# Convolution leaving two neighbouring rows in a partition, a second stage on 64-row halves and seven weight buffers in a spectral-mix kernel

## The chip, the cores and the metric

The kernel runs on one core of a Trainium2 chip. The metric is the device time of one execution in microseconds (us). Before the change the median of three runs is 230.59 us. The engines are named as in the profile: PE is the matrix engine's matmuls, PEld its weight loads (they can overlap PE), DVE the vector engine, ACT the scalar engine, POOL the general-purpose engine, which here mostly issues loads, and SP the engine that issues the stores. Every matmul result lands in PSUM, which this kernel holds as four tiles Z[0] to Z[3] of two banks each.

## The reference

Inputs: x of shape (8, 3264, 192) in float32 (B batches, S rows, D columns), weight (8, 7), and, called moe_ below, w_r and w_i (64, 192, 192) and w_ch (192, 192). In short:

```python
w = softmax(weight, axis=-1)                       # 8 heads, 7 taps
u0 = causal 7-tap convolution of x along S         # 24 columns of D per head
X = rfft(u0, axis=1)                               # along S
Y[:, :64] = complex product of X[:, :64] with w_r + i w_i, a 192x192 matrix per mode
y = irfft(Y, n=S, axis=1)
u = u0 + y
out = u + maximum(u @ w_ch, 0)                     # float32
```

Only the first 64 modes are used, so both transforms are matmuls with small cosine and sine tables. The kernel works in bf16 with float32 accumulation.

## The kernel before, in words

**Layout.** The order of instructions on each engine is the order in which the program writes them (manual_schedule); what waits for what follows from tiles that are written and read. A sequence of 3264 rows is cut into NF = 25 tiles of 128 rows and a half tile of 64; batches go in NQ = 4 pairs q, i being the batch in the pair. xall (L58) holds x, and later the convolved u0, as [128 rows, slot, i, 192].

**Stage 1: load, convolution, forward transform (L115 to L289).** load_unit (L115) loads the row tiles of a unit from x with POOL's queue, casting to bf16, with one DMA per batch of the pair (L121). The work is cut into 24 units (L47 to L49), six for each pair, of 2, 4 or 5 row tiles. The set-up builds the taps by a softmax, seven masks (L147), and a banded matrix `band` of 128 x 256 per head: L168 writes each tap into a packed form under a mask, L174 and L176 copy that to the band. The cosine and sine tables `ftab` follow: products L151, reduction L153, L158, L177 and L178 on DVE, then Sin, Abs and Sin on ACT (L180 to L182). conv_half (L219) convolves a unit for four heads: four matmuls with the main band (L228) and four with the band's spill into the next tile (L234), each with 128 output rows and n x 2 x 24 moving columns (192 for four tiles, 240 for five); L237 does the half tile. ACT (L242) or DVE (L244) copies the bank pair back into xall. conv_half uses Z[0] and Z[1], one each. dft_unit (L246) accumulates the forward transform of a unit in Z[2], one matmul of 384 columns per tile (L250; L254 for the half tile), one unit behind the convolution; when a pair is done, xtrans (L259) turns the result with twelve matmuls that use the two column halves of the array, L264 on columns 0 to 63 and L266 on 64 to 127 (`tile_position`), and DVE copies it to mixa (L271) for the mixing.

**Stage 2: mixing per mode and transposes (L292 to L390, L499 to L516).** The weights w_r and w_i come in NG = 16 groups of four modes; load_w (L294) loads one group with two DMAs on POOL's queue (L297) into one of five buffers. mix (L361) does the twelve small matmuls of a group (L366) and then issues the load of the group that takes the same buffer, g + 5. mix_copy (L371) and mix_trans (L374) bring the result to `yet`. Between the mixes stand the transposes which the last stage needs, in 49 jobs: g_bank (L318, transposes of the tables L321), cm_bank (L324, columns 0 to 127 of u0, L329, with L334 for the half tile) and ct_bank (L336, columns 128 to 191 of two batches stacked, L340, with L347 for the half tile). A job fills one bank of Z[0] or Z[1] with up to eight transposes, and one copy of 128 x 1024 takes it out: `copy` (L306) gives every third to ACT (L309), the others to DVE (L311). next_bank (L313) goes around the four banks of those two tiles. `some(4)` and `some(3)` (L508, L514) put seven jobs after each two mixes. The first matmuls of the output's first two items are put between and after the last mixes.

**Stage 3: output (L392 to L539).** An item is a duo: two row tiles of a pair of batches, one in each bank of a Z tile. z_pieces (L392) lists the matmuls of a tile: "c" is u0 @ w_ch (with `cm` and wm over 64 of the 128 columns at a time, and `ct` with wt2 for the last 64 columns), "g" is the inverse transform's contribution to u @ w_ch, with `zw`'s first half, "y" the inverse transform itself with its second half. `both` (L418) issues the pieces of the two tiles in turn on two row halves of the array, rows 0 to 63 and 64 to 127, the matmul being L436: 12 of 192 moving columns and 8 of 384 per item. When the halves swap banks, a nop (L424) waits for the last matmuls before. relu (L458, ACT) makes maximum(u @ w_ch, 0) in PSUM between the "g" and the "y" pieces, finish (L461) adds u0 (DVE, L478) into an output buffer in `arena` and stores it with two DMAs on SP, one per batch (L486) or per tile (L491). Of the seven output buffers each holds one item. zw_pair (L441) makes `zw` for one pair of batches from `yet`: four matmuls and two scaled copies (DVE L450, ACT L452). Two zw_pairs stand ahead of the loop, and two inside it after items 13 and 26 (L538). One item in the 51 takes the four half tiles together ("h").

Of the kernel before, what the change touches and what calls it, by code (L numbers as in the profile page):

```python
# [9 lines left out]
ALU = mybir.AluOpType  # L10
# [9 lines left out]
def kernel(  # L20
# [21 lines left out]
    TAIL = D - P  # L42
# [4 lines left out]
    UNITS0 = ((0, 2), (2, 4), (6, 5), (11, 5), (16, 5), (21, 5))  # L47
    UNITS = ((0, 5), (5, 5), (10, 4), (14, 4), (18, 4), (22, 4))
    units = [(q, t0, n) for q in range(NQ) for t0, n in (UNITS if q else UNITS0)]  # L49

# [6 lines left out]

    xall = sb("xall", [NSLOT, 2, D], BF16)  # L58
    cm = sb("cm", [NQ, 2 * NF + 1, P], BF16)
    ct = sb("ct", [NQ, NT, P], BF16)  # L60
    ftab = sb("ftab", [NT + 1, 2 * MODES], BF16)
    yet = sb("yet", [2, B, 2 * MODES], BF16)
    mixa = sb("mixa", [3 * (MODES + 1) * 2 * B], BF16)
    xt = mixa[:, :].rearrange("p (j m k) -> p j m k", j=3, m=MODES + 1)
    zw = mixa[:, 0:2 * B * D].rearrange("p (t b d) -> p t b d", t=2, b=B)
    band = sb("band", [H, 2 * P], BF16)
    wm = sb("wm", [2 * D], BF16)
    w1 = sb("w1", [2 * D], BF16)
    wt2 = sb("wt2", [D], BF16)
    ident = sb("ident", [P], BF16)  # L70
    perm = sb("perm", [P], BF16)
    ascale = sb("ascale", [1], F32)
    halfpi = sb("halfpi", [1], F32)
    xs = [sb(f"xs{i}", [2, D], BF16) for i in range(2)]
    ymix = [sb(f"ymix{i}", [2, D], BF16) for i in range(2)]
    NW = 5
    WGB = 4 * 3 * D
    arena = sb("arena", [NW * WGB], BF16)
    wts = [arena[:, WGB * i:WGB * (i + 1)].rearrange("p (m j e) -> p m j e", m=4, j=3) for i in range(NW)]
    NO = 7  # L80
    OB = 2 * 2 * 2 * D
    outs = [arena[:, OB * i:OB * (i + 1)].bitcast(F32).rearrange("p (k d) -> p k d", k=2) for i in range(NO)]
# [8 lines left out]
    NTM = NT + 1  # L91
    kprod = temp(NTM * MODES, F32)
    turns = temp(NTM * MODES, F32)
# [8 lines left out]
    cidx = temp(PW, F32)  # L102
    masks = temp(KK * PW, U16)
    sidx = temp(NTM, F32)
# [7 lines left out]
    def slot(q, t):  # L112
        return NT * q + t

    def load_unit(q, t0, n):  # L115
        nf = min(n, NF - t0)
        s0 = slot(q, t0) + 1
        for i in range(2):
            off = ((2 * q + i) * S + P * t0) * D
            src = bass.AP(tensor=x.tensor, offset=x.offset + off, ap=[[D, P], [P * D, nf], [1, D]])  # L120
            nc.gpsimd.dma_start(out=xall[:, s0:s0 + nf, i, :], in_=src)  # L121
# [5 lines left out]
    load_unit(*units[0])  # L127
    nc.gpsimd.iota(sidx[:, 0:NT], pattern=[[P, NT]], base=0, channel_multiplier=1,
                   allow_small_or_imprecise_dtypes=True)
    nc.gpsimd.iota(sidx[:, NT:NTM], pattern=[[1, 1]], base=P * NF - HALF, channel_multiplier=1,  # L130
                   allow_small_or_imprecise_dtypes=True)
    nc.gpsimd.iota(midx, pattern=[[1, MODES]], base=0, channel_multiplier=0,
                   allow_small_or_imprecise_dtypes=True)
    for g in range(4):
        nc.gpsimd.iota(cidx[32 * g:32 * g + 32, :], pattern=[[1, PW]], base=0, channel_multiplier=-1,
                       allow_small_or_imprecise_dtypes=True)
    load_unit(*units[1])
    hs = [xall[HALF:P, NT:NSLOT:NT, 0, :], xall[0:HALF, NT:NSLOT:NT, 1, :]]
    nc.vector.memset(halfpi[:], math.pi / 2)
    nc.vector.memset(ascale[:], 2.0 / S)  # L140
    nc.vector.memset(ascale[0:1, :], 1.0 / S)
    nc.vector.memset(ascale[64:65, :], 1.0 / S)
    for a in hs:
        nc.vector.memset(a, 0.0)
    nc.vector.memset(band[:], 0.0)
    for k in range(KK):
        nc.vector.tensor_scalar(out=masks[:, PW * k:PW * (k + 1)], in0=cidx,  # L147
                                scalar1=float(KK - 1 - k), scalar2=None, op0=ALU.is_equal)
    kp3 = kprod.rearrange("p (t m) -> p t m", t=NTM)
    tu3 = turns.rearrange("p (t m) -> p t m", t=NTM)  # L150
    nc.vector.tensor_tensor(out=kp3, in0=sidx.unsqueeze(2).to_broadcast([P, NTM, MODES]),  # L151
                            in1=midx.unsqueeze(1).to_broadcast([P, NTM, MODES]), op=ALU.mult)
    nc.vector.tensor_scalar(out=turns, in0=kprod, scalar1=1.0 / S, scalar2=MAGIC, op0=ALU.mult, op1=ALU.add)  # L153
# [4 lines left out]
    nc.vector.tensor_scalar(out=turns, in0=turns, scalar1=-MAGIC, scalar2=float(S), op0=ALU.add, op1=ALU.mult)  # L158
# [7 lines left out]
    nc.vector.memset(packed, 0.0)  # L166
    for k in range(KK):
        nc.vector.copy_predicated(out=pk3,  # L168
                                  mask=masks[:, PW * k:PW * (k + 1)].unsqueeze(1).to_broadcast([P, H, PW]),
                                  data=ta3[:, :, k:k + 1].to_broadcast([P, H, PW]))  # L170
# [6 lines left out]
    nc.vector.tensor_tensor(out=kprod, in0=kprod, in1=turns, op=ALU.subtract)  # L177
    nc.vector.tensor_scalar(out=kprod, in0=kprod, scalar1=-float(S) / 2, scalar2=float(S) / 2,  # L178
# [6 lines left out]
    for q, t0, n in units[2:5]:  # L185
        load_unit(q, t0, n)
# [12 lines left out]
    for q, t0, n in units[5:9]:  # L199
        load_unit(q, t0, n)  # L200
# [10 lines left out]
    for q, t0, n in units[9:]:  # L211
        load_unit(q, t0, n)
# [86 lines left out]

    for g in range(NW):  # L300
        load_w(g)
# [268 lines left out]
```

## Time and profile before

| what | value |
|---|---|
| runs | 231.66, 230.59, 227.48 us; median 230.59 |
| the profiled execution: span from its first to its last instruction | 230.0 us |
| mean granted PE clock | 0.916 |
| busy: PE, PEld | 167.9 us (73%), 125.9 us (55%) |
| busy: DVE, ACT, POOL | 131.1 us (57%), 96.5 us (42%), 67.5 us (29%) |
| moved | 40.03 MB, mean 174 GB/s |
| convolution L228, L234: matmuls, busy | 192 and 192, 26.4 and 26.1 us |
| forward transform L250 | 100, 20.6 us |
| output matmuls L436 | 1048 in three groups, 112.0 us |
| output add L478 on DVE | 50, mean 958 ns |
| relu L459 on ACT | 51, mean 795 ns |
| store on SP | 102, 192.0 KB each, 3.1 us from issue to landing |

The profile is one execution. Its slices cut the span into 40 equal parts of 5.75 us; a digit is the busy share of an engine in tenths (9 means 90% or more), PEclk the clock that PE was granted in tenths of full speed, DMA the mean busy share of the 16 DMA engines, GB/s what they moved. A row of the timeline gives the start of a run of equal instructions in us, the busy time, the engine, the line, the operation, output <- inputs with their shape and type, how many instructions there were (x32), and in square brackets the idle time ahead with what ended it. A row of the chain of waits gives the start, the time that the chain spent there, the engine, tile and line, and how many instructions. The chain goes back from the last instruction to whatever released it each time. Matmuls are pipelined, so the sum of their durations counts overlap; in the text their price is taken from start to start.

### The profile page before, as it was taken

The numbers are of one execution on the slowest core, as the hardware profiler recorded it, in microseconds if no ns is written. First come the engines' busy times: TensorE is split into PE (matmuls) and PEld (weight loads), VectorE is DVE, ScalarE is ACT, GpSimd is POOL, SyncE is SP. The second block draws the span as 40 slices with busy tenths as digits, with TensorE's granted clock in tenths as the row PEclk, the third lists the DMA queues.
The fourth block names the chain that finished last, engine by engine and source line by source line (L and its number), as shares of the span: only waits on it lengthen the run. The fifth ranks groups of instructions, "written<-read, shape, count | busy, mean of one in ns | idle before, by whom it ended". The sixth has DMA issues, their size and how long they took to land.

```text
span 230.0 us, 5494 instructions
## 1 busy us (share of the span) xinstructions
PE 167.9 (73%) x2303; PEld 125.9 (55%) x2303; DVE 131.1 (57%) x177; ACT 96.5 (42%) x123; POOL 67.5 (29%) x115
## 2 busy tenths in 40 slices
PE   0010999899799836665866666869989997999960
PEld 0010888688687715654755565426646655666730
DVE  6991254845758463345344452335776776877690
ACT  2039334424343310423443244236655665666540
POOL 7999996775730004044034200000000000000000
PEclk9999999999999995589589769599999999999996
DMA  3999999999999004879998860004799997799997
GB/s 43 157 184 188 190 190 191 189 192 189 173 197 206 10 0 64 144 105 153 157 136 133 146 104 0 3 0 126 246 313 286 303 308 236 240 315 310 309 276 250
DMA packets 63912, 40.03 MB, mean 174 GB/s; under 512 B 29584, under 2 KB 63888, under 8 KB 63888
## 3 DMA queue, kind: packets, MB, share of 16 engines
q0 software_dynamic: 36000, 19.59, 63.6%
q1 hardware_dynamic: 27888, 20.09, 28.3%
q8 instruction: 18, 0.29, 0.5%
q14 instruction: 6, 0.05, 0.1%
HBM read 39.20 MB, written 20.05 MB: 258 GB/s over the span
## 4 chain that ended last, share of the span: by engine, by line
PE 53%; POOL 14%; DVE 12%; DMA 10%; ACT 5%; issue 4%; DVEq 0%; POOLq 0%; ACTq 0%
PE z L436 28%; POOL xall L121 11%; DMA xall<-in_x_dram 10%; PE z L329 7%; PE z L340 4%; DVE cm L311 3%; PE z L366 3%; PE z L228 2%; DVE mixa L271 2%; PE z L234 2%; PE z L250 2%; DVE xall L244 2%; PE z L321 1%; ACT cm L309 1%; DVE ct L311 1%
## 5 line engine op out<-in xcount | busy, mean ns | idle before, releaser
L478 DVE TENSOR_TENSOR arena<-z,xall 128x768 f32<-128x768 f32 x50 | 47.8, 958 | 18.2 <-ACT z L459 10.6
L436 PE MATMUL z<-mixa,ftab 64*128 64x384 bf16 (+1 forms) x432 | 51.1, 317 | 1.7 <-ACT z L459 0.8
L459 ACT ACTIVATE z<-z 128x768 f32<-128x768 f32 x51 | 40.5, 795 | 24.5 <-PE z L436 24.5
L228 PE MATMUL z<-xall,band 128*128 128x192 bf16 (+2 forms) x192 | 26.4, 263 | 25.5 <-ACT band L174 15.1
L244 DVE CAST xall<-z 128x768 bf16<-128x768 f32 (+2 forms) x24 | 25.1, 1047 | 29.6 <-PE z L234 18.7
L121 POOL DMA_DIRECT2D xall<-in_x_dram x48 | 39.5, 840 | 6.6 <-DMA xall<-in_x_dram 5.0
L436 PE MATMUL z<-wm,cm 64*128 64x192 bf16 x408 | 34.9, 250 | 3.1 <-ACT mixa L452 2.7
L242 ACT CAST xall<-z 128x768 bf16<-128x768 f32 (+2 forms) x24 | 20.4, 851 | 34.7 <-PE z L234 24.8
L228 PEld LDWEIGHTS <-band 128*128 128x128 bf16 x192 | 17.9, 102 | 29.1 <-ACT band L174 15.1
L436 PEld LDWEIGHTS <-cm 64*128 64x128 bf16 x408 | 15.9, 95 | 24.5 <-PE z L436 14.6
L329 PE MATMUL z<-ident,xall 128*128 128x128 bf16 x208 | 19.3, 257 | 10.6 <-DVE cm L311 5.8
L297 POOL DMA_DIRECT2D arena<-in_moe_w_r_dram x16 | 10.1, 629 | 54.8 <-PE z L366 53.5
L234 PE MATMUL z<-xall,band 128*128 128x192 bf16 (+2 forms) x192 | 26.1, 257 | 0.0
L436 PE MATMUL z<-wt,ct 64*128 64x192 bf16 x208 | 26.0, 247 | 0.0
L329 PEld LDWEIGHTS <-xall 128*128 128x128 bf16 x208 | 16.4, 117 | 13.3 <-issue 12.0
L436 PEld LDWEIGHTS <-ftab 64*128 64x128 bf16 x432 | 19.7, 94 | 3.9 <-issue 2.2
L311 DVE COPY cm<-z 128x1024 bf16<-128x1024 bf16 (+1 forms) x19 | 11.7, 627 | 17.5 <-PE z L329 17.3
L250 PE MATMUL z<-xall,ftab 128*128 128x384 bf16 x100 | 20.6, 330 | 0.4 <-DVE xall L244 0.4
L234 PEld LDWEIGHTS <-band 128*128 128x128 bf16 x192 | 18.2, 102 | 0.6
L271 DVE CAST mixa<-z 128x384 bf16<-128x384 f32 x8 | 13.6, 1877 | 2.1 <-PE z L266 2.1
L340 PE MATMUL z<-ident,xall 128*64 128x128 bf16 x208 | 9.6, 245 | 6.8 <-DVE cm L334 2.9
L309 ACT COPY cm<-z 128x1024 bf16<-128x1024 bf16 (+1 forms) x9 | 9.1, 1006 | 12.7 <-PE z L329 12.7
(89 smaller groups left out, 160.8 us busy)
## 6 DMA issues: line engine op xcount, KB each, us to landing
out_dram<-arena SPq DMA_DIRECT2D x102, 192.0 KB, 3.1
arena<-in_moe_w_r_dram POOLq DMA_DIRECT2D x16, 288.0 KB, 6.0
arena<-in_moe_w_i_dram POOLq DMA_DIRECT2D x16, 288.0 KB, 6.8
xall<-in_x_dram POOLq DMA_DIRECT2D x18, 240.0 KB, 6.8
xall<-in_x_dram POOLq DMA_DIRECT2D x22, 192.0 KB, 8.4
xall<-in_x_dram POOLq DMA_DIRECT2D x6, 144.0 KB, 7.5
xall<-in_x_dram POOLq DMA_DIRECT2D x4, 96.0 KB, 4.1
wm<-in_moe_w_ch_dram POOLq DMA_DIRECT2D x1, 48.0 KB, 6.8
```

The costliest lines, as they stand in the source:

```text
L121: nc.gpsimd.dma_start(out=xall[:, s0:s0 + nf, i, :], in_=src)
L228: nc.tensor.matmul(o, band[:, h, 0:P], xall[:, s0 + 1:s0 + 1 + n, :, dsl], start=(j % 2 == 0), stop=False, skip_group_check=True)
L234: nc.tensor.matmul(o[:, k0:n, :, :], band[:, h, P:2 * P], xall[:, s0 + k0:s0 + n, :, dsl], start=False, stop=not last, skip_group_check=True)
L242: nc.scalar.copy(out=dst, in_=srcv)
L244: nc.vector.tensor_copy(out=dst, in_=srcv)
L250: nc.tensor.matmul(xp, ftab[:, t, :], xall[:, slot(q, t), :, :], start=(t == 0), stop=False, skip_group_check=True)
L311: nc.vector.tensor_copy(out=out, in_=in_)
L329: nc.tensor.transpose(tp[:, P * k:P * k + P], xall[:, slot(q, t), i, 0:P], ident[:])
L340: nc.tensor.transpose(tp[64 * i:64 * i + 64, P * k:P * k + P], xall[:, slot(q, t0 + k), i, P:D], ident[:], tile_position=(0, 64 * i))
L436: mm = nc.tensor.matmul(zt[:, bank, cols], l, r, start=(begin and k == 0), stop=(end and k == len(lst) - 1), skip_group_check=True)
L459: nc.scalar.activation(out=zt[:, :, 0:2 * D], in_=zt[:, :, 0:2 * D], func=ACT.Relu)
L478: nc.vector.tensor_tensor(out=o[:, :, :], in0=zt[:, :, 0:2 * D], in1=xall[:, s[0]:s[1] + 1:s[1] - s[0], :, :].rearrange("p k i d -> p k (i ...
```

## The change

The layout of rows changes for the whole kernel. The convolution writes row 2p + j of a group of 256 rows into partition p, slot j, so a partition holds two neighbouring rows, and the pair of rows of one batch is 1536 contiguous bytes of the output.

- Set-up: one mask in place of seven; the band is made of 32-column writes; the memset of `packed` comes ahead; the table has 26 groups instead of 27; its steps become the functions table_a to table_d, table_sin and table_cos. They are issued between the copies of the first convolution rounds. Sine and cosine are two ACT instructions each.
- Stage 1: 12 units, each of 4 or 5 groups of 256 rows, loaded by fewer and larger DMAs. conv_round does two heads at a time, four rounds per unit, with 16 matmuls of 64 output columns each, whose stationary operand is the band at stride 2, and which go to the two column halves of the array in turn. Z[0], Z[1] and Z[2] take the rounds in turn, and the copies alternate between ACT and DVE. The forward transform uses Z[3] and runs up to three units behind at the start. xtrans's two copies to mixa are in a contiguous order, one on DVE and one on ACT.
- Stage 2: the three columns 3p + j of a row are turned at a time, so that 384 columns of two batches fill three transposes of 128 x 128: ct_job, 40 jobs, and g2_job for the tables, 7 jobs, 47 in all. cm, cm_bank and ct_bank go. The stationary operand of ct_job has stride 3. Two of every five copies go to ACT. Weights have seven buffers, of which four lie in the part of `ct` that the last pair's jobs fill; wslot lists the buffer of each group, and a load is issued after the mix that used its buffer last. Two jobs, xtrans and two more jobs stand ahead of the first mix. zw is made in two halves of 32 modes each, zw_low for all four pairs after mix 9, the other half after mix 15. Mixes 14 and 15 are copied and turned singly, with the first matmuls of items 0 and 1 between.
- Stage 3: 52 items, an item being a group of 256 rows of both batches. z_c and z_y issue its 28 matmuls, all of 192 moving columns, in turn on the two row halves; each row half keeps to its own bank, and the nop goes. finish adds and stores with one DMA of 384 KB; there are six output buffers. zw_pair and the half-tile item go: the last item of each pair has 96 partitions (PT) instead of 128.

```diff
-    UNITS0 = ((0, 2), (2, 4), (6, 5), (11, 5), (16, 5), (21, 5))
-    UNITS = ((0, 5), (5, 5), (10, 4), (14, 4), (18, 4), (22, 4))
+    UNITS = ((0, 4), (4, 4), (8, 5))
+    UNITS_LAST = ((0, 5), (5, 4), (9, 4))
...
+    c3 = (NQ - 1) * NT * 3 * P
+    wplace = [ctf[:, c3 + WGB * k:c3 + WGB * k + WGB] for k in range(4)]
+    wplace += [arena[:, WGB * k:WGB * k + WGB] for k in range(NWA)]
+    wslot = [0, 1, 2, 3, 4, 5, 6, 0, 1, 4, 5, 6, 4, 5, 6, 4]
+    zplace = [arena[:, NWA * WGB + OB * k:NWA * WGB + OB * k + OB] for k in range(NZ)]
...
-    for k in range(KK):
-        nc.vector.tensor_scalar(out=masks[:, PW * k:PW * (k + 1)], in0=cidx,
-                                scalar1=float(KK - 1 - k), scalar2=None, op0=ALU.is_equal)
+    nc.vector.tensor_scalar(out=mask, in0=cidx, scalar1=0.0, scalar2=None, op0=ALU.is_equal)
...
+        o = KK - 1 - k
+        nc.vector.copy_predicated(out=pk3[:, :, o:o + 32],
+                                  mask=mask.unsqueeze(1).to_broadcast([P, H, 32]),
+                                  data=ta3[:, :, k:k + 1].to_broadcast([P, H, 32]))
...
+    def table_sin():
+        for h in range(2):
+            nc.scalar.activation(out=fview[:, :, h, 1, :], in_=half_of(kp3, h), func=ACT.Sin, scale=-TWOPI / S)
+        nc.scalar.activation(out=tu3, in_=kp3, func=ACT.Abs)
+    def table_cos():
+        for h in range(2):
+            nc.scalar.activation(out=fview[:, :, h, 0, :], in_=half_of(tu3, h), func=ACT.Sin, scale=-TWOPI / S,
+                                 bias=halfpi[:, 0:1])
...
-    def conv_half(q, t0, n, half):
...
+    def conv_round(q, t0, n, r):
+        z = Z[czn[0] % 3]
+        odd = czn[0] % 2
+        czn[0] += 1
+        s0 = cslot(q, 2 * t0)
+        for hh in range(2):
+            h = 2 * r + hh
+            dsl = slice(GRP * h, GRP * h + GRP)
+            o = z[:, hh, 0:4 * GRP * n].rearrange("p (t j c) -> p t j c", t=n, j=2)
+            for j in range(2):
+                for c in range(2):
+                    nc.tensor.matmul(o[64 * c:64 * c + 64, :, j, :].rearrange("p t (i e) -> p t i e", i=2),
+                                     band[:, h, j:P:2], xall[:, s0 + 1 + c:s0 + 1 + c + 2 * n - 1:2, :, dsl],
+                                     start=(j == 0), stop=False, tile_position=(0, 64 * c), skip_group_check=True)
+            for j in range(2):
+                for c in range(2):
+                    k0 = 1 if (t0 == 0 and c == 0) else 0
+                    nc.tensor.matmul(o[64 * c:64 * c + 64, k0:n, j, :].rearrange("p t (i e) -> p t i e", i=2),
+                                     band[:, h, P + j:2 * P:2],
+                                     xall[:, s0 + c + 2 * k0:s0 + c + 2 * n - 1:2, :, dsl],
+                                     start=False, stop=True, tile_position=(0, 64 * c), skip_group_check=True)
+        dst = xall[:, s0:s0 + 2 * n, :, 48 * r:48 * r + 48].rearrange("p s i (h e) -> p h (s i) e", h=2)
+        srcv = z[:, :, 0:4 * GRP * n].rearrange("p h (c e) -> p h c e", e=GRP)
+        if odd:
+            nc.vector.tensor_copy(out=dst, in_=srcv)
+        else:
+            nc.scalar.copy(out=dst, in_=srcv)
...
+            dst = mixa[:, :].rearrange("p (k b c) -> p k b c", k=4, b=B)[:, :, b, :]
+            srcv = z[:, i, 0:3 * P].rearrange("p (k c) -> p k c", k=4)
+            if i == 0:
+                nc.vector.tensor_copy(out=dst, in_=srcv)
+            else:
+                nc.scalar.copy(out=dst, in_=srcv)
...
-    for k, u in enumerate(units):
...
+    steps = {(0, 0): [table_a], (0, 1): [table_b], (0, 2): [table_c], (0, 3): [table_d, table_sin], (1, 0): [table_cos]}
+    LAG = 3
+    done = 0
+    pend = None
+    for k, u in enumerate(units):
+        for r in range(4):
+            conv_round(*u, r)
+            for f in steps.get((k, r), []):
+                f()
+            if pend is not None and r == 0:
+                xtrans(pend)
+                pend = None
+            if r == 1:
+                lim = k if k > LAG else (k - 2 if k == LAG else 0)
+                while done < lim:
+                    dft_unit(*units[done])
+                    if units[done][1] + units[done][2] == NTT:
+                        pend = units[done][0]
+                    done += 1
+    for g in range(7):
+        load_w(g)
...
-        if ncopy[0] % 3 == 0:
+        if ncopy[0] % 5 in (2, 4):
...
-    def cm_bank(q, b0, n):
...
-    def ct_bank(q, t0, n):
...
+    def ct_job(q, k0, n):
+        tp = next_bank()
+        for k in range(n):
+            g, j = divmod(k0 + k, 3)
+            src = xall[:, cslot(q, g), :, :].rearrange("p i (k j) -> p (i k) j", j=3)[:, :, j]
+            nc.tensor.transpose(tp[:, P * k:P * k + P], src, ident)
+        o = (q * NT * 3 + k0) * P
+        copy(ctf[:, o:o + P * n], tp[:, 0:P * n])
+    def g2_job(g0, n):
+        tp = next_bank()
+        for k in range(n):
+            for c in range(2):
+                for i in range(2):
+                    nc.tensor.transpose(tp[64 * i:64 * i + 64, P * (2 * k + c):P * (2 * k + c) + P],
+                                        ftab[:, g0 + k, 64 * c:64 * c + 64], ident, tile_position=(0, 64 * i))
+        copy(tabs[:, 2 * P * g0:2 * P * (g0 + n)], tp[:, 0:2 * P * n])
...
+    def zw_mm(q, h, z):
+        for t, w in ((0, wm), (1, w1)):
+            for i in range(2):
+                lhs = yet[:, t, h, :, :, :].rearrange("p c m b -> p (c m) b")[:, :, 2 * q + i]
+                nc.tensor.matmul(z[64 * i:64 * i + 64, 0:2 * D], lhs, w, start=(t == 0), stop=(t == 1),
+                                 tile_position=(0, 64 * i), skip_group_check=True)
+    def zw_copy(q, h, z, act=False):
+        for t in range(2):
+            dst, srcv = zw[:, h, q, t, :], z[:, D * t:D * t + D]
+            sc = ascale[:, 0:1] if h == 0 else 2.0 / S
+            if act:
+                nc.scalar.activation(out=dst, in_=srcv, func=ACT.Copy, scale=sc)
+            else:
+                nc.vector.tensor_scalar(out=dst, in0=srcv, scalar1=sc, scalar2=None, op0=ALU.mult)
+    def zw_low(q):
+        k = tb[0] % 4
+        tb[0] += 1
+        z = Z[k // 2][:, k % 2, :]
+        zw_mm(q, 0, z)
+        zw_copy(q, 0, z, act=(q % 2 == 1))
...
-    def both(duo, zt, first, which, begin=False, end=False):
...
+    def z_c(it, z):
+        q, t = it
+        for j in range(2):
+            for k in range(3):
+                for i in range(2):
+                    mm(z, i, j, ct[rows(i), q, 2 * t + j, k, :], w3[rows(i), k, :], start=(j == 0 and k == 0))
+    def z_y(it, z, which, halves, stop=False):
+        q, t = it
+        for j in range(2):
+            for h in halves:
+                for i in range(2):
+                    mm(z, i, j, g2[rows(i), 2 * t + j, h, :], zw[rows(i), h, q, which, :], stop=stop)
...
+        o = outs[n % NO]
+        s0 = cslot(q, 2 * t)
+        nc.vector.tensor_tensor(out=o[0:pn, :, :].rearrange("p i (j d) -> p i j d", j=2),
+                                in0=z[0:pn, :, 0:2 * D].rearrange("p i (j d) -> p i j d", j=2),
+                                in1=xall[0:pn, s0:s0 + 2, :, :].rearrange("p j i d -> p i j d"), op=ALU.add)
+        dst = bass.AP(tensor=out.tensor, offset=out.offset + (2 * q * S + 2 * P * t) * D,
+                      ap=[[2 * D, pn], [S * D, 2], [1, 2 * D]])
+        nc.sync.dma_start(out=dst, in_=o[0:pn, :, :])
...
-    for d in range(NG // 2):
...
+    some(2)
+    xtrans(NQ - 1)
+    some(2)
+    for g in range(NG):
+        mix(g)
...
+        if g >= 14:
+            mix_copy([g])
+            if g == 14:
+                z_c(seq[0], Z[0])
+                z_y(seq[0], Z[0], 0, (0,))
+            mix_trans([g])
+            if g == 14:
+                z_c(seq[1], Z[1])
+                z_y(seq[1], Z[1], 0, (0,))
+            continue
+        if g % 2 == 1:
+            mix_copy([g - 1, g])
+            some(2)
+            mix_trans([g - 1, g])
+            some(2)
+        else:
+            some(4)
+        for w in range(7, NG):
+            prev = max(k for k in range(w) if wslot[k] == wslot[w])
+            if prev == g:
+                load_w(w)
+        if g == 9:
+            for q in range(NQ):
+                zw_low(q)
+        if g == 13:
+            some(99)
+    hi = [Z[2][:, 0, :], Z[2][:, 1, :], Z[3][:, 0, :], Z[3][:, 1, :]]
+    zw_mm(0, 1, hi[0])
+    zw_copy(0, 1, hi[0])
+    for q in range(1, NQ):
+        zw_mm(q, 1, hi[q])
+        zw_copy(q, 1, hi[q])
+    for n in range(N + 2):
+        if n < N and n >= 2:
+            z_c(seq[n], Z[n % 4])
+        if n >= 2:
+            z_y(seq[n - 2], Z[(n - 2) % 4], 1, (0, 1), stop=True)
+            finish(n - 2, Z[(n - 2) % 4])
+        if n < N:
+            z_y(seq[n], Z[n % 4], 0, (1,) if n < 2 else (0, 1))
+            relu(Z[n % 4])
```

## The prediction, made before the changed kernel ran

> **What bounds the kernel now.** I read the page's slices first, then busy time by window, then the timeline of each stage. The page splits the span into three stages with different limits.
>
> ```profile
> PE   0010999899799836665866666869989997999960
> PEclk9999999999999995589589769599999999999996
> DMA  3999999999999004879998860004799997799997
> GB/s 43 157 184 188 190 190 191 189 192 189 173 197 206 10 0 64 144 105 153 157 136 133 146 104 0 3 0 126 246 313 286 303 308 236 240 315 310 309 276 250
> ```
>
> Slices of 5.75 us: PE is nearly full to slice 14 (the load and convolution stage) and again from slice 28 (the output stage). Between them PE is at 6 or 8, its clock drops to half, and DMA is half idle: no resource is full there. In windows (PE, PEld, DVE, ACT, POOL, clock, DMA share, GB/s):
>
> ```profile
> 40.00:60.00 20.00, 18.54 (x197) 15.30 (x196) 13.72 (x12) 7.59 (x10) 13.31 (x20) 1.00 1.58 188
> 120.00:148.00 28.00, 18.00 (x308) 14.48 (x307) 11.61 (x23) 10.20 (x15) 3.69 (x6) 0.80 0.54 84
> 200.00:222.00 22.00, 21.64 (x366) 14.54 (x361) 17.14 (x19) 13.46 (x18) 0.00 (x0) 1.00 1.01 312
> ```
>
> Stage 1 ends with the last L254 at 82.46, stage 2 with the start of the last twelve L366 at 148.07, stage 3 at 230.0. x (10.0 MB as bf16, at about 0.19 MB/us) is in by about 59 us, so at 82 PE is the late one: it started steady work only at 23.1. Why stage 2 is slow shows in its timeline:
>
> ```profile
> 102.70 1.08 PE L340 MATMUL z<-ident,xall 128*64 128x128 bf16 x32 [0.73 <-DVE cm L334]
> 103.54 1.34 ACT L309 COPY ct<-z 128x1024 bf16<-128x1024 bf16 x1
> 103.83 0.69 DVE L311 COPY ct<-z 128x1024 bf16<-128x1024 bf16 x1 [0.54 <-PE z L340]
> 104.57 0.64 PE L340 MATMUL z<-ident,xall 128*64 128x128 bf16 x16 [0.78 <-DVE ct L311]
> ```
>
> PE fills two banks, then stands until a copy has ended. In the built program the second bank of a Z tile waits for the copy of the first, so four banks act as two tiles: PE, copy, PE, copy in turn. Stage 3 is one item after the other, 1.22 us apart by the adds, with PE full:
>
> ```profile
> 158.04 0.96 DVE L478 TENSOR_TENSOR arena<-z,xall 128x768 f32<-128x768 f32 x1 [0.28 <-PE z L436]
> 159.05 0.12 PEld L436 LDWEIGHTS <-cm 64*128 64x128 bf16 x4 [0.29 <-PE z L436]
> 159.26 0.96 DVE L478 TENSOR_TENSOR arena<-z,xall 128x768 f32<-128x768 f32 x1 [0.27 <-PE z L436]
> ```
>
> The chain of waits, in order of time, shows two holes of about 2.1 us in it, after 170.80 and 188.98, where zw_pair sits:
>
> ```profile
> 155.80 15.00 PE z L436 x242
> 172.93 16.05 PE z L436 x260
> 191.07 28.40 PE z L436 x478
> ```
>
> **Stage 1, 82.5 to 77.2.** Prices of one matmul, from start to start in the timeline: 82 ns at 192 columns (four L234 0.49, one 0.25), 102 at 240, 162 at 384. The convolution now issues 768 matmuls of 64 output columns instead of 384 of 128, in pairs on two column halves. The nearest row is the pair L264/L266:
>
> ```profile
> 70.36 0.22 PE L264 MATMUL z<-ident,xs 128*64 128x128 bf16 x1
> 70.36 0.22 PE L266 MATMUL z<-perm,xs 128*64 128x128 bf16 x1
> 70.41 0.22 PE L264 MATMUL z<-ident,xs 128*64 128x128 bf16 x1
> 70.41 0.22 PE L266 MATMUL z<-perm,xs 128*64 128x128 bf16 x1
> ```
>
> Two start together and the next two 0.055 us later, what one matmul of 128 columns takes, though each has its own weight load (stride 3, as the new ones have stride 2). So a pair costs what a single one did: 82 or 102 ns. Bounds: 82 for a pair, 164 if they run in turn. I take 82, the shown row.
> Band: ahead of it go L153 (1.44), L158 (1.05) and six of seven L147 (0.66); L168 shrinks from 304 to 256 elements (3.55 to about 3.1). Band is ready at 11.2 instead of 15.06. The table steps now stand between the first conv copies: DVE runs them to 19.9 (3 copies and 5.5 us of steps, from 10.8, waiting for PE twice), then ACT has sine 1.8, Abs 1.6, the copy of unit 1's first round, cosine 1.8 and the next copy, to 26.6. With three Z tiles PE may be only two rounds ahead, so it ends unit 2 at about 30.4, with no DFT done. Left for PE: six units of 32 pairs x 82 (15.7), three of 32 x 102 (9.8), 104 DFT matmuls x 162 (16.8), three xtrans (1.2), 22 changes of tile shape x 0.1 (L266 to L250: 2.2), the last copy (1.1): 46.8, so 77.2. If the table chain costs nothing it is 73; if PE also stays at half clock to 34, 80. The 1.88 us mixa copies (L271) that stalled PE 1.18 us three times become contiguous ones, 0.62 by L450. POOL's fewer, larger loads hide behind DMA at 9 tenths; without that cover each costs its 0.84 us issue.
> The rule against this: the Trainium skill, TensorEngine Tiling, Restrictions and Gotchas, says that column tiling gives up Fast Weight Load, and TensorE: Matmul & The Clock Gate, LDWEIGHTS, gives P/1.2 ns, 53 for 64 columns. Two loads in turn would be 107 ns a pair, 5.3 us more in stage 1 and 224.8 in all (an estimate from those pages); the row's 0.055 us with two loads in it speaks for overlap.
>
> **Stage 2, 148.07 to 146.6.** Before: mix pairs start at 87.08, 97.35 ... 146.15, 8.4 us per seven transpose jobs, 1.21 a job with all around it. The new jobs have the same size (8 transposes, one 128x1024 copy; 0.69 on DVE, 1.04 on ACT) and the same two-tile wait, 47 instead of 49. I keep 1.21; all at full clock it would be 1.0, all at half 1.4. Four jobs and the last xtrans precede mix 0: 5.4 us, so mix 0 at 82.6. Mix 9 follows 36 jobs later (43.4). Then four jobs (4.8) with zw_low (four matmul-copy turns, 3.8), mix 10, three jobs, mix 11: 55.6 after mix 0. Seven buffers cover groups 0 to 6 and the slots of 0 and 1 again; but groups 12 to 15 reuse slots, and 15 is issued only after mix 12. A lone group issued at 130.84 had moved by 136.2, 5.4 us; two in a row take about 8. So the last mix stands at 64 after mix 0: 146.6, some 6 us of it a new wait for weights. POOL has nothing else queued.
>
> **Stage 3, 81.9 to 72.1 us.** Before: 7.7 to the steady rhythm (155.80), 65.9 to the last relu, 8.3 from there to the end. After: start 6.0 (shorter yet and zw copies, eight of 0.35 on DVE; bounds 5 and 7.7). A step has 14 pairs of 192 columns, 14 x 82 = 1.15 us; before 6 x 82 and 4 x 162 plus a nop wait. The 28 loads of 64x128 per step run in pairs beside the matmuls, as before in the three c pairs. DVE's add 0.96 and ACT's relu 0.80 fit under 1.15. 50 full steps 57.5, the first two 0.3, tail 8.3: 72.1. The late zw_pairs and the 64-row item are gone.
> Stores go from two of 192 KB to one of 384 KB a step; SP issues 52 instead of 102, hidden.
>
> ```profile
> q1 hardware_dynamic: 27888, 20.09, 28.3%
> ```
>
> 28.3% of 16 x 230 us over 27888 packets is 37.3 ns for 768 bytes. At the same price per packet a step's 256 packets take 0.60 us, at twice 1.195, at the best slice's 315 GB/s 1.25. I take them as hidden, nearest the middle; the ends cost 0 and 5 us.
> The Trainium skill, DMA: Bandwidth & Descriptors, Specifications, asks 512 bytes for line rate, which 768 already has; then doubling gains nothing per byte, and by that rule the sum is 2.3 us longer, 221.8.
>
> **Sum.** 82.6 + 64 + 72.1 = 218.7 of span, against 230.0. The median of the three runs shown is 230.59 (227.48 to 231.66), 0.6 above the span; so 219.3, call it 219.5.
>
> **Rivals.**
> Slower: column pairs run in turn. The convolution has accumulating matmuls on strided moving rows, which L264 has not. Then 192 x 82 + 96 x 102 = 25.5 us more: 245. It passes the old time from 38 ns extra a pair; held to one load's 123 ns it would be 10 us, 229.5.
> Stores bound stage 3: DMA stands at 9 in the slices, PE will ask 342 GB/s and 315 is the most seen. 2.3 to 5 us: 222 to 224.5. Against: half the packets.
> Stage 2 gets longer: more copies on the slower ACT, clock at half for longer; 43 jobs x 0.14: 225.5 to 227.
> Stage 2 gets shorter: jobs at full clock, 1.0 each, 8 to 9 us less: 211.
>
> **Chances.** Forecast 0.50 (own range 214 to 226), pairs in turn 0.16, stores 0.12, longer stage 2 0.13, shorter 0.09. Two per cent (226.0 to 235.2) is about what a measurement can tell here. Faster: 0.46 + 0.09 + 0.09 + 0.03 = 0.67; same: 0.04 + 0.03 + 0.10 + 0.05 = 0.22; slower 0.11, all from the pairs. Range 210 to 231, which leaves out most of the slow rival and the tails.
>
> **What will show it.** Pairs of conv matmuls starting together, 82 ns apart; unit 2 done near 30; last DFT near 77; two mixes 9.7 us apart; PE waiting for weights before mixes 13 to 15; adds 1.15 apart; 8 us from the last relu to the end. A conv pair at 160 ns, adds at 1.25 or more, or jobs at 1.35 would make it wrong.

## The result and the profile after

The changed kernel takes 244.28 us in the median of four runs (243.84 to 245.02); the kernel before took 230.89 beside it. The ratio is 1.064, with a 95% interval of 1.053 to 1.075: it is slower by 6%, where 219.5 us had been forecast. The profiled execution has a span of 243.3 us. In its lines L279 and L285 are the convolution, L300 the forward transform, L371 and L380 the transposes of ct_job and g2_job, L357 and L359 their copies on ACT and DVE, L393 the mix, L407 the turn of its result, L423 zw, L447 the output's matmuls, L467 the relu and L474 the add.

The page's slices, of 6.08 us each, show where the time went:

```profile
PE   0181999999998566766867767756699999999980
PEclk9998699999999855555555555556679999999997
DMA  6999999999999066005643015395038999989995
```

The stages at both ends are full, as before. Between them lie slices 14 to 28, in which PE is at 5 to 8 and its clock at half almost without a break; before the change the clock of that stage came and went. Set against the forecast by its own landmarks:

| landmark | forecast | measured | later by, in this stretch |
|---|---|---|---|
| last forward transform matmul | 77.2 | 78.4 | 1.2 |
| mix 0 | 82.6 | 84.6 | 0.8 |
| mix 9, 36 jobs on | 126.0 | 142.4 | 14.4 |
| last mix | 146.6 | 169.0 | 6.0 |
| end of the span | 218.7 | 243.3 | 2.2 |

The five add up to the 24.6 us by which the span differs. 20.4 of it lie between mix 0 and the last mix, in the middle stage.

The convolution's pairs did what the forecast took from the row of xtrans. In the timeline four matmuls of L279 and then four of L285 start every 0.16 us, so a pair costs 0.08:

```profile
19.36 0.36 PE L279 MATMUL z<-xall,tabs 128*64 128x192 bf16 x4 [2.01 <-DVE xall L292]
19.52 0.36 PE L285 MATMUL z<-xall,tabs 128*64 128x192 bf16 x4
19.68 0.36 PE L279 MATMUL z<-xall,tabs 128*64 128x192 bf16 x4
```

The output stage too: the adds stand 1.15 us apart, and 7.8 us lie between the start of the last relu (235.45) and the end.

```profile
195.91 0.96 DVE L474 TENSOR_TENSOR arena<-z,xall 128x768 f32<-128x768 f32 x1 [0.20 <-ACT z L467]
197.06 0.96 DVE L474 TENSOR_TENSOR misc<-z,xall 128x768 f32<-128x768 f32 x1 [0.20 <-ACT z L467]
198.22 0.96 DVE L474 TENSOR_TENSOR misc<-z,xall 128x768 f32<-128x768 f32 x1 [0.20 <-ACT z L467]
```

In the middle stage the chain of waits (start, length, what) reads:

```profile
83.62 1.01 PE z L371 x8
84.62 0.61 PE z L393 x12
85.23 0.98 PE z L371 x8
...
86.30 0.70 DVE ct L359
...
87.05 1.88 PE z L371 x16
...
88.95 1.02 ACT ct L357
...
90.01 1.01 PE z L371 x8
91.03 0.61 PE z L393 x9
91.64 0.98 PE z L371 x8
```

Two banks are filled in one go, then PE stands for a copy, and so on. The mix (L393) lies each time in the middle of the two fills, where PE would have been busy anyway, and not in the stall. That follows from the count: four jobs stand between two mixes, the stall comes after every second job, and four jobs ahead of mix 0 set the phase for good. Before the change seven jobs stood between two pairs of mixes, so every other pair fell into a stall. The clock of the kernel before rose at 99.13, 116.19 and 136.67, each time after such a pair (97.35, 113.66 and 129.85). At the first of them its timeline has no gap from 95.56 to 99.82:

```profile
95.56 1.86 PE L329 MATMUL z<-ident,xall 128*128 128x128 bf16 x16 [0.78 <-DVE cm L311]
97.35 1.15 PE L366 MATMUL z<-arena,mixa 128*32 128x192 bf16 x24
98.44 1.38 PE L329 MATMUL z<-ident,xall 128*128 128x128 bf16 x16
```

What that does to the clock shows in windows of 3.41 us, laid on the trace's own changes of clock: every stretch of one granted clock that ends inside the kernel is a whole multiple of 3.41 us (6.83, 54.61 and 85.33 in the changed kernel). The columns are the window, its length, busy PE, PEld, DVE, ACT and POOL with counts, the granted clock, DMA share, GB/s. First the kernel before:

```profile
92.30:95.71 3.41, 1.91 (x17) 1.75 (x17) 1.76 (x3) 1.38 (x2) 0.00 (x0) 0.50 1.19 197
95.71:99.12 3.41, 3.41 (x47) 2.90 (x46) 0.69 (x1) 1.49 (x2) 0.78 (x2) 0.50 0.17 28
99.13:102.54 3.41, 1.74 (x28) 1.55 (x26) 1.60 (x4) 1.01 (x1) 1.67 (x3) 1.00 0.87 126
```

The window without a gap (3.41 of 3.41 busy) is followed by the full clock. Then the changed kernel:

```profile
76.51:79.92 3.41, 1.91 (x16) 1.37 (x17) 0.91 (x2) 1.18 (x2) 0.00 (x0) 1.00 0.73 123
79.92:83.33 3.41, 1.71 (x28) 1.46 (x28) 1.00 (x3) 1.37 (x2) 0.00 (x0) 1.00 0.00 0
83.34:86.75 3.41, 2.58 (x28) 1.91 (x28) 0.67 (x2) 1.12 (x2) 1.20 (x2) 0.50 0.00 0
...
90.16:93.57 3.41, 2.44 (x28) 1.77 (x27) 0.69 (x1) 1.41 (x2) 1.22 (x2) 0.50 0.21 30
...
96.99:100.40 3.41, 2.63 (x31) 1.96 (x29) 0.69 (x1) 1.01 (x1) 0.00 (x0) 0.50 0.00 0
```

After two windows of 0.56 and 0.50 the clock falls at 83.34, and it stays at half for 85.3 us: no window until 165 is busy for more than 2.63 of 3.41, which is 0.77. Half a clock makes a fill take 1.01 us instead of 0.46 (in the same chain at 78.72, before the clock fell), and with that the stage feeds on itself: PE works longer, yet stands often enough never to reach the share that would bring the clock back.

### The profile page after: what moved, and what is told of

It is laid out like the page before. It is cut to its first block, busy times and chain, and to the rows that moved or that the text cites. A ratio compares the mean times of both kernels' runs of the same rounds, so it can differ in the third digit from the quotient of the medians.

```text
span 243.3 us, 6877 instructions
## 1 busy us (share of the span) xinstructions
PE 186.8 (77%) x3048; PEld 159.7 (66%) x3048; DVE 113.2 (47%) x158; ACT 100.6 (41%) x136; POOL 50.7 (21%) x83
## 3 DMA queue, kind: packets, MB, share of 16 engines
q1 hardware_dynamic: 14032, 20.09, 23.1%
## 4 chain that ended last, share of the span: by engine, by line
PE 73%; DVE 12%; ACT 6%; issue 3%; DMA 2%; POOL 0%; DVEq 0%
PE z L447 26%; PE z L371 15%; PE z L279 8%; PE z L300 7%; PE z L285 7%; PE z L393 3%; DVE ct L359 3%; ACT ct L357 3%; PE z L380 3%; DMA arena<-in_moe_w_i_dram 2%; PE z L423 2%; DVE mixa L433 1%; DVE arena L191 1%; PE z L407 1%; DVE xall L292 1%
## 5 line engine op out<-in xcount | busy, mean ns | idle before, releaser
L371 PE MATMUL z<-misc,xall 128*128 128x128 bf16 x312 | 38.0, 301 | 18.1 <-DVE ct L359 9.7
L467 ACT ACTIVATE z<-z 128x768 f32<-128x768 f32 x52 | 41.2, 795 | 24.3 <-PE z L447 24.3
L279 PE MATMUL z<-xall,tabs 128*64 128x192 bf16 (+1 forms) x384 | 37.2, 270 | 17.8 <-ACT tabs L197 11.5
L371 PEld LDWEIGHTS <-xall 128*128 128x128 bf16 x312 | 31.5, 140 | 24.3 <-issue 24.1
L447 PE MATMUL z<-mixa,tabs 64*128 64x192 bf16 x832 | 45.0, 247 | 0.6 <-ACT z L467 0.6
L292 DVE CAST xall<-z 128x768 bf16<-128x768 f32 (+1 forms) x23 | 23.4, 1018 | 35.7 <-PE z L285 35.1
L279 PEld LDWEIGHTS <-tabs 128*64 128x64 bf16 x384 | 24.7, 118 | 21.3 <-ACT tabs L197 11.5
L474 DVE TENSOR_TENSOR arena<-z,xall 128x768 f32<-128x768 f32 (+1 forms) x36 | 34.2, 956 | 9.1 <-ACT z L467 7.7
L447 PEld LDWEIGHTS <-tabs 64*128 64x128 bf16 x832 | 36.6, 96 | 1.3 <-issue 1.3
L359 DVE COPY ct<-z 128x1024 bf16<-128x1024 bf16 (+1 forms) x24 | 16.2, 675 | 45.1 <-PE z L371 45.1
L285 PE MATMUL z<-xall,tabs 128*64 128x192 bf16 (+2 forms) x384 | 36.7, 264 | 0.0
L447 PE MATMUL z<-w,ct 64*128 64x192 bf16 x624 | 36.7, 251 | 0.0
L447 PEld LDWEIGHTS <-ct 64*128 64x128 bf16 x624 | 28.4, 98 | 0.8 <-issue 0.7
L357 ACT COPY ct<-z 128x1024 bf16<-128x1024 bf16 (+1 forms) x16 | 16.0, 999 | 29.4 <-PE z L371 29.3
L285 PEld LDWEIGHTS <-tabs 128*64 128x64 bf16 x384 | 25.8, 118 | 0.0
L300 PE MATMUL z<-xall,tabs 128*128 128x384 bf16 (+1 forms) x104 | 18.8, 327 | 1.5 <-ACT xall L294 0.9
L474 DVE TENSOR_TENSOR misc<-z,xall 128x768 f32<-128x768 f32 x16 | 15.3, 958 | 3.3 <-ACT z L467 3.3
L300 PEld LDWEIGHTS <-tabs 128*128 128x128 bf16 (+1 forms) x104 | 9.4, 98 | 8.6 <-issue 1.7
```

Source lines behind the costliest of these rows:

```text
L279: nc.tensor.matmul(o[64 * c:64 * c + 64, :, j, :].rearrange("p t (i e) -> p t i e", i=2), band[:, h, j:P:2], xall[:, s0 + 1 + c:s0 + 1 + c ...
L285: nc.tensor.matmul(o[64 * c:64 * c + 64, k0:n, j, :].rearrange("p t (i e) -> p t i e", i=2), band[:, h, P + j:2 * P:2], xall[:, s0 + c + 2 ...
L292: nc.vector.tensor_copy(out=dst, in_=srcv)
L300: nc.tensor.matmul(xp, ftab[0:kk, g, :], xall[0:kk, cslot(q, g), :, :], start=(g == 0), stop=(g == NT - 1), skip_group_check=True)
L357: nc.scalar.copy(out=out, in_=in_)
L359: nc.vector.tensor_copy(out=out, in_=in_)
```

## The experiments

The theory: the middle stage is slow because its windows stay below a share of about 0.8 at half clock (**clock theory**). Its rivals: more copies on ACT, and transposes with strided weights (**copy theory**); late weights (**weights theory**). The expectations stand as they were put down before each run. "Per job" is the time from mix 0 to mix 9 over the 36 jobs between; for the two kernels built on the one before it is the time between the first and the last pair of mixes that have jobs between them, over those jobs (49, and 48 in b_even). The mean clock is that of the time from the last forward transform to the last mix.

| kernel | us | span | per job | mean clock, middle stage |
|---|---|---|---|---|
| before | 230.89 | 230.0 | 1.21 | 0.76 |
| changed | 244.28 | 243.3 | 1.61 | 0.53 |
| a_phase | 217.63 | 215.9 | 1.04 | 0.88 |
| a_dummy | 223.03 | 221.3 | 1.15 | 0.95 |
| a_dummy2 | 227.48 | 225.7 | 1.26 | 0.86 |
| b_even | 249.82 | 247.7 | 1.48 | 0.57 |
| a_copy3 | 243.60 | 241.8 | 1.58 | 0.53 |
| a_w9 | 241.65 | 239.9 | 1.61 | 0.53 |
| a_order | 206.48 | 204.7 | 0.81 | 0.94 |
| b_order | 213.29 | 212.0 | 0.85 | 0.93 |
| a_order_w9 | 202.40 | 200.8 | 0.81 | 0.97 |
| a_order_w9_hi | 198.19 | 196.9 | 0.81 | 0.97 |

The kernel before took 229.83 to 235.33 us beside these runs. Where no interval is given, a kernel ran once, or (a_order_w9, 199.28 to 202.53) its four runs lie too far apart for one.

**a_phase: one job moved.**

```diff
     some(2)
     xtrans(NQ - 1)
-    some(2)
+    some(1)
```

> The changed kernel with one transpose job fewer ahead of mix 0 (three instead of four); the same job is done later, no work is left out. Clock theory: PE is granted the full clock only after a window of 3.41 us in which it was busy for at least about 0.8 (in the profile before the change the clock rose after windows of 0.80 to 1.00, in the changed kernel the windows of the second stage reach 0.77 at most), and every second job leaves PE standing for 0.8 to 1.1 us, until a copy has ended. With three jobs ahead the mixes and the turns of their results fall into these stalls, windows reach 0.85, the clock comes back for part of the stage as before the change: 225 to 238 us, mean granted clock of the second stage 0.65 to 0.85 instead of 0.5. Rival, copy theory: the stage is long because more copies are on ACT (two in five) and the transposes load strided weights, and the clock only follows; order changes nothing: 242 to 245 us. Rival, weights theory: the waits for late weights set the end: 242 to 245 us.

217.63 us, below the range that the clock theory had set, and 25 us below both rivals. The timeline shows the mix and the turn where the stall was:

```profile
86.38 1.86 PE L371 MATMUL z<-misc,xall 128*128 128x128 bf16 x16 [0.85 <-DVE ct L359]
...
88.18 0.68 PE L393 MATMUL z<-ct,mixa 128*16 128x192 bf16 x12
...
89.35 1.87 PE L371 MATMUL z<-misc,xall 128*128 128x128 bf16 x16 [0.49 <-ACT ct L357]
...
91.01 0.63 PE L407 MATMUL z<-misc 128*128 128x128 bf16 x4
```

The stall ahead of 89.35 is 0.49 instead of 1.1, and the windows say what follows:

```profile
86.16:89.57 3.41, 2.69 (x31) 2.21 (x31) 0.86 (x2) 1.29 (x2) 0.40 (x1) 0.50 0.93 157
89.58:92.99 3.41, 2.74 (x27) 2.57 (x25) 0.92 (x2) 1.28 (x3) 0.81 (x2) 0.50 0.73 111
92.99:96.40 3.41, 2.14 (x41) 1.81 (x39) 1.85 (x3) 1.01 (x1) 0.00 (x0) 1.00 0.37 62
```

After 0.79 the clock stayed at half, after 0.80 it rose: a narrow margin, in the only run of this kernel. From 92.99 it stays full for 44 us although the windows are then busy for only 0.56 to 0.75, until one of 0.25 ends it. PE's idle time before the transposes, while it waits for copies, goes from 20.5 us to 13.5. So of the 27.4 us of span about 7 are stalls that the mixes now fill; that the rest goes with the clock is a subtraction here, which the next two runs bear out.

**a_dummy and a_dummy2: more work.** Six, then two, useless transposes after every second job (idle_work is called at the end of ct_job and of g2_job), into PSUM columns that nobody reads; the rest of the kernel is the changed one.

```diff
+    def idle_work():
+        if tb[0] % 2 == 1:
+            for k in range(6):
+                nc.tensor.transpose(ZB[3][:, k % 2, 512 + P * (k // 2):640 + P * (k // 2)], ident, ident)
...
+        idle_work()
```

> The changed kernel with six useless transposes after every second job, written to columns of PSUM that nobody reads: more work for PE, in the place where it stands and waits for a copy. Nothing is left out. Clock theory: PE's windows in the second stage go from 0.77 to above 0.9, the clock rises to full, a job costs about 1.0 us instead of 1.6, and the kernel with more work is faster: 218 to 232 us. Copy theory and weights theory: 244 us or a few us more.

> The changed kernel with two useless transposes after every second job instead of the six of the run before. Clock theory with a point of about 0.8: two add 0.25 us of PE work at half clock to some 3.2 us, so the windows of 0.68 to 0.77 go to 0.76 to 0.85, the clock rises within the stage but falls back more often than with six: 222 to 236 us. If the gain came not from the clock passing a point but in proportion to the useless work: a third of the 21 us of the run with six, 237 us or more.

223.03 and 227.48 us: with six the kernel that does more is 21 us faster, with two 17 us faster. A third of the work brings four fifths of the gain, which fits something with a point better than something in proportion, although the six also cost more PE time themselves. The windows of the run with two:

```profile
91.02:94.43 3.41, 2.52 (x31) 1.99 (x30) 0.69 (x1) 1.49 (x2) 1.22 (x2) 0.50 0.22 23
94.43:97.84 3.41, 2.86 (x32) 2.48 (x34) 1.38 (x3) 0.37 (x2) 0.00 (x0) 0.50 0.89 150
97.84:101.25 3.41, 2.14 (x40) 1.75 (x33) 1.29 (x2) 1.92 (x2) 0.00 (x0) 1.00 0.00 0
```

One window at 0.84 (2.86 of 3.41) lifts the clock, and it holds until 145.6. In these runs nothing is removed from the chain of fills and copies, and PE waits for weights as long as in the changed kernel (3.1 and 3.5 us, there 3.1), so only the clock can have paid. This is the cleanest of the proofs.

**b_even: the fault put into the kernel before.**

```diff
-            some(3)
+            some(4)
```

> The kernel before the change with eight transpose jobs after each two mixes instead of seven; the same 49 jobs in the same order, used up sooner. Clock theory: with an even number the mixes always fall between the two tiles, where PE does not stand, the windows stay under 0.8, the clock stays at half as in the changed kernel until the jobs are used up, and the kernel is slower: 236 to 250 us. Copy theory and weights theory: nothing changes but the place of some jobs: 228 to 233 us.

249.82 us, 16 us slower than the kernel before beside it, and 0.2 below the upper end of the range. Its slices have the changed kernel's picture, with one island of full clock after a window that came to 0.90:

```profile
PE   0012999898998466777567676679997997999970
PEclk9999999999999955558755555555899999999996
```

**a_copy3 and a_w9: the rivals by themselves.** Every third copy on ACT as before; nine weight buffers, the two new ones in an unused part of the arena.

```diff
-        if ncopy[0] % 5 in (2, 4):
+        if ncopy[0] % 3 == 0:
```

```diff
-    NWA = 3
-    NZ = 3
+    NWA = 5
+    NZ = 0
...
-    wslot = [0, 1, 2, 3, 4, 5, 6, 0, 1, 4, 5, 6, 4, 5, 6, 4]
+    wslot = [0, 1, 2, 3, 4, 5, 6, 7, 8, 4, 5, 6, 7, 8, 4, 5]
...
-    for g in range(7):
+    for g in range(9):
...
-        for w in range(7, NG):
+        for w in range(9, NG):
```

> The changed kernel with every third copy on ACT, as before the change, instead of two of five. Clock theory: where a stall waits for DVE instead of ACT it is about 0.3 us shorter, some three stalls fewer on ACT, so 1 to 2 us less, 241 to 244 us, as long as the windows stay under 0.8; if one passes it, a few us more are gained. Copy theory: three or four of 19 copies go from 1.0 to 0.69 us and the pace of the jobs follows: 236 to 240 us with the clock still at half.

> The changed kernel with nine weight buffers and the old order of the banks. The weights theory in its own right: the waits ahead of the last mixes (0.5 and 2.6 us in the profile, and the start of mix 14 that they push back) go, the rest of the stage stays at half clock: 238 to 241 us. If weights were the main cause of the loss: 228 to 234 us.

243.60 and 241.65 us, the middle clock 0.53 in both. Against the changed kernel's median the copies are worth 0.7 us, which is less than the spread of that kernel's runs (1.2), and the weights 2.6. a_w9 stays just above its range: PE has no wait for weights left, and the way from mix 9 to the last mix takes 23.4 us instead of 26.7, which is little more than the 3.1 us of those waits. Neither is the cause of the 14.4 us between mixes 0 and 9, where both kernels keep the pace of the changed one. The strided weight loads are in every kernel built on the changed one, so a_phase rules them out.

**a_order and b_order: the stall taken away.** The four banks are taken in the order 0, 2, 1, 3, so that neighbouring jobs lie in different tiles. In a_order the same line stands also in zw_low, which takes its bank from the same counter.

```diff
-        k = tb[0] % 4
+        k = (0, 2, 1, 3)[tb[0] % 4]
```

> The changed kernel with the four banks of the transposes taken in the order 0, 2, 1, 3, so that neighbouring jobs lie in different tiles and PE can fill one tile while the other is copied. No work is left out. Clock theory: PE has no stall at half clock (two fills take 2.0 us, a copy 0.7 to 1.0), so the clock rises to full; then a job takes 0.75 to 1.0 us and the last mix starts at 125 to 145 instead of 169, perhaps held up by weights: 203 to 222 us. Copy theory: the copies, 0.69 us on DVE and 1.0 on ACT, set the pace as before: 236 to 245 us. Weights theory: 236 to 245 us, the waits only get longer.

> The kernel before the change with the banks of the transposes in the order 0, 2, 1, 3. The stall goes there too: 49 jobs at about 0.9 us instead of 1.21, clock mostly full, five weight buffers as before: 213 to 222 us. If the rest of the change (first stage 4 us shorter, output stage 7 us shorter) is worth what the profiles show, it stays 8 to 14 us above the changed kernel in the same order (206.5); if the rest is worth nothing, it comes to 204 to 209.

206.48 us, and 213.29 for the kernel before with the same line changed (ratio to it 0.917, 0.910 to 0.925). In a_order the copies run beside the fills, a fill of eight every 0.7 us or so, and the clock stays up until the jobs are used up (it falls at 123.3):

```profile
88.79 2.00 PE L371 MATMUL z<-misc,xall 128*128 128x128 bf16 x24
89.43 0.69 DVE L359 COPY ct<-z 128x1024 bf16<-128x1024 bf16 x1 [0.70 <-PE z L371]
90.13 1.01 ACT L357 COPY ct<-z 128x1024 bf16<-128x1024 bf16 x1 [0.69 <-PE z L371]
90.82 0.69 DVE L359 COPY ct<-z 128x1024 bf16<-128x1024 bf16 x1 [0.70 <-PE z L371]
91.19 0.61 PE L371 MATMUL z<-misc,xall 128*128 128x128 bf16 x8 [0.41 <-ACT ct L357]
```

With the same order in both the rest of the change can be priced, by the spans: 5.1 us less to mix 0 (82.1 against 87.2), 5.2 more from there to the last mix (48.4 against 43.2), 7.4 less to the end (74.2 against 81.6). That is 7.3 us gained, 6.8 by the times, and less than the 8 to 14 that had been expected. The second term says that the new middle stage is no better by itself; without its waits for weights (a_order_w9) it is 44.4, still not shorter than 43.2.

**a_order_w9 and a_order_w9_hi: the best version.** Nine weight buffers as above on a_order, then also the second half of zw in turn on two tiles and two engines.

```diff
-    hi = [Z[2][:, 0, :], Z[2][:, 1, :], Z[3][:, 0, :], Z[3][:, 1, :]]
+    hi = [Z[2][:, 0, :], Z[3][:, 0, :], Z[2][:, 1, :], Z[3][:, 1, :]]
...
-        zw_copy(q, 1, hi[q])
+        zw_copy(q, 1, hi[q], act=(q % 2 == 1))
```

> The changed kernel in the order 0, 2, 1, 3 and with nine weight buffers, the two new ones in a part of the arena that was unused, so that the load of group 15 is issued after mix 10 instead of mix 12. The waits for weights before the last mixes (3.4 us in the run with the order alone) go, and with them the fall of the clock at 123 us: 198 to 203 us. If the waits are hidden by something else: 205 to 207 us.

> The one with nine buffers, and the second half of zw made in the order Z2, Z3, Z2, Z3 with every second copy on ACT, since each of its four matmul groups waited 0.8 us for the copy before: 1.5 to 2.5 us less than with nine buffers alone, 196.5 to 201 us. If the clock or the first items hide it: the same as with nine buffers.

202.40 and 198.19 us. The last is 0.852 of the kernel before (0.845 to 0.859), so it beats both kernels. In a_order_w9 the waits for weights are gone, but the fall of the clock at 123 us, which was to go with them, is still there, for 3.4 us instead of 6.8. The new order of zw shortens the way from the last mix to the third relu from 9.0 us to 6.3; that is 2.7 of the 4.2 us between the two medians, and the fastest run of a_order_w9 is only 1.1 above. In the slices of the last version the clock drops once in the middle, after the jobs have ended:

```profile
PEclk9999969999999999999999999699999999999998
```

## Why the prediction was wrong

**Stage 1: right.** Pairs at 0.08 us, the third unit's last convolution matmul started at 30.3 where its end was forecast for 30.4, the first convolution matmul at 11.47 against 11.2, the end 1.2 us late. The rival "column pairs run in turn", the only one that was given a slower kernel, did not happen; that its 245 us lie so near the measured 244.28 is chance. The estimate for loads in turn, 0.107 us a pair (the Trainium skill, TensorE: Matmul & The Clock Gate, LDWEIGHTS), did not come about either.

**Stage 2: the step that failed is "I keep 1.21; all at full clock it would be 1.0, all at half 1.4".** The changed kernel took 1.61 us a job, with the clock of its middle stage at a mean of 0.53, where the kernel before had 0.76. The 1.21 was a mean over two clocks, and what mixes them is where the mixes lie among the jobs. The new jobs do have the old size and the old two-tile wait, as the step said; the number of jobs between mixes, which the change made even, was not looked at. The forecast had both facts in hand, the stall after every second job and "four jobs" between mixes, and did not lay the one upon the other. The upper bound, for which the prediction gives no working, was wrong as well: at a mean clock near half the kernel before takes 1.48 (b_even) and the changed one 1.61. The sign "two mixes 9.7 us apart" came out as 12.9. The rival "stage 2 gets longer: clock at half for longer" named the right mechanism; its price, 0.14 us a job, should have been 0.40, and 36 jobs of it are the 14.4 us in the table. The rival's other half, more copies on ACT, is not it (a_copy3). With one job moved (a_phase) the kernel comes to 217.63, within 2 us of the forecast, but at 1.04 us a job and not at 1.21, so this does not confirm the price.

**The weights: mechanism right, too large.** PE stood 0.5 us for weights before mix 13 and 2.6 before mix 14, not some 6, and not before mix 15; the gap between mixes 9 and 10 was 11.6 us and not the 8.6 of the sum (4.8 and 3.8). The 6.0 us that this stretch lost are the half clock and the stalls, and not the weights: without any wait for weights it still takes 23.4 us at half clock (a_w9), and 15.3 with the other order of the banks (a_order_w9), where the forecast less its 6 us of waiting leaves 14.6.

**Stage 3: right, with a late start.** The adds are at 1.15, the stores hidden, the tail 7.8 against 8.3. The way from the last mix to the third relu took 9.3 us, where the sum has about 7.5 (6.0, 0.3 and one step of 1.15). Two of the four groups of zw matmuls waited 0.8 us for a copy, and the clock fell once more at 172.1; in the last version the same way takes 6.3.

## What to carry to other kernels

When an engine's clock goes up and down in a stage, a mean time per job from that stage isn't a price: look which order of work lets it rise, and whether the change keeps it. Lay every periodic stall (here after two jobs) against the period of what stands between (here seven jobs, then four): work that falls into the stalls is nearly free, and work that falls beside them costs its full time. And where two buffers share a tile that is waited for as a whole, go around the tiles before the banks; that order was worth 18 us on the kernel before and 38 on the changed one.

## What the runs showed of the hardware

The stores became cheaper per byte with the larger packets, though the output stage did not need it. The row of their queue in the changed kernel:

```profile
q1 hardware_dynamic: 14032, 20.09, 23.1%
```

23.1% of 16 x 243.3 us is 899 us of engine time for the 20.09 MB, where the kernel before took 28.3% of 16 x 230.0 us, 1042: about 14% less per byte. Over the packets of the queue, a few of which are small, that is 64 ns each against 37.

The granted clock of PE changes on a grid of 3.41 us. From half it rose after windows in which PE was busy for 0.80 (a_phase, before), 0.84 (a_dummy2), 0.89 (the changed kernel at 165.3) and more, and in none of the twelve traces did it rise from a stretch at half after less than 0.80; it stayed at half after 0.77 to 0.79. But four windows above that did not lift it: 0.81 and 0.82 (a_dummy2 at 84.2, before at 129.85), and 0.96 and 0.91 in b_even at 161.4 and 168.2:

```profile
161.39:164.80 3.41, 3.28 (x42) 1.60 (x39) 0.22 (x1) 1.19 (x2) 0.00 (x0) 0.50 0.02 5
164.80:168.21 3.41, 2.29 (x10) 0.96 (x9) 0.82 (x2) 0.71 (x1) 0.00 (x0) 0.50 0.00 0
168.22:171.63 3.41, 3.12 (x14) 0.79 (x14) 1.11 (x2) 2.06 (x4) 0.00 (x0) 0.50 0.00 0
```

So a share of about 0.8 was needed for every rise and was not always enough. Why is open; the ends of the matmuls are modelled, so this share is not exact. From full it fell after windows of up to 0.55, but some of 0.51 to 0.56 (before at 99.1, the changed kernel at 76.5) did not bring it down: where that point lies stays open too.

The Trainium skill, TensorE: Matmul & The Clock Gate, What's actually happening, gives full clock after a busy window of about 3.4 us and half after an idle one. The length agrees with the 3.41 us. The fall does not agree: at 83.34 the clock fell though PE had not stood for more than 1.1 us at a time and was busy for half of the window. The same page, A second HAM failure mode: psum-queue depth-cycling, describes going around PSUM banks with small stops that make the clock swing; here the stops were so regular that it did not swing but stayed at half for 85 us.
